# GpSimd instead of VectorE for the subtraction that makes wo_l, in an attention and softplus feed-forward kernel on one Trainium2 core

## The chip, the cores and the metric

The kernel runs on one core of a Trainium2 chip. The metric is the device time of one execution in microseconds (us). An engine is named as in the profile: PE is TensorE's matmul (PEld its weight load), DVE is VectorE, ACT is ScalarE, POOL is GpSimd, SP is SyncE, which only issues DMAs here.

## The reference

Eight batches of eight heads, with 576 rows of 64. A first softmax attention lets 32 packed queries p look at k and v; a second one lets q look at the 32 packed results. The heads are put side by side, which gives x of 4608 rows and 512 columns, and a feed-forward part with softplus follows.

```python
p_packed = sm_attn(p, k, v)
out = sm_attn(q, p_packed, p_packed)
x = attn_out.transpose(0, 2, 1, 3).reshape(B * S, H * D)
h = x @ w_in                                        # 512 x 2048
g = np.maximum(h, 0.0) + np.log1p(np.exp(-np.abs(h)))
return (g @ w_out).astype(np.float32)               # 2048 x 512
```

The weights w_in and w_out are float64; everything else is float32.

## The kernel before

**The work.** For each batch b the attention is computed first. Its last products aT (the weights of the second softmax) are split into a rounded high part at_h (ScalarE, L545) and a low part at_l (VectorE, L546). The feed-forward part runs over 16 slices f of 128 columns of w_in; one (b, f) is called a unit. `make_m` multiplies the packed results into w_in (PE psm, L563) and splits the product into mh (ScalarE, L578) and ml (VectorE, L579); for batch 0 one call serves two units. `gemm1` (PE ph, L600) makes h of the unit in two halves of 288 columns with three products, high by high, high by low and low by high. `softplus` takes |h| (ScalarE L622), exp (L624), ln (L625), adds max(h, 0) (VectorE L627, reading PSUM), lets GpSimd copy the last 64 columns aside (L631) and splits the rest into gh (VectorE L614) and gl (L615). Two units later `gemm2_tile` (L638) adds gh·wo_h, gh·wo_l and gl·wo_h into PSUM. The unit f+1 of gemm1 overwrites the PSUM that L627 of unit f has read, so PE waits for it.

**The conversion.** The float64 weights are turned into float32 bits on the chip, in the generator `convert`, one step for each of 16 slices of w_in (i0 to i15) and 16 of w_out (o0 to o15), in the order i0 i1 o0 o1 i2 i3 o2 o3 and so on. A step has these instructions, all on tiles of 128x512:

- a DMA of the float64 slice into one of four places (L156, on SP's queue)
- ScalarE makes m from the high words (L200) and r from the low words (L204)
- VectorE makes t from m in two instructions (L206: the sign; L211: shift and or)
- GpSimd adds t and r as integers (L219), which rounds; for w_in the sum goes to w_in_sb, for w_out it stays in r
- for w_out only: ScalarE rounds t to wo_h (L238), and the subtraction r - wo_h makes wo_l (L244)

The tiles m, r and t come from rings of one or two buffers, in the first steps also from the softplus tiles. So the r of a later step (L204, on ScalarE) has to wait until the last reader of an earlier r is done: the add for w_in, the subtraction for w_out.

**What sets the order.** PE's order is the program's own. On the other engines a scheduler puts the instructions of the generators in order when the program is built; each engine then runs its queue strictly in that order. The main loop calls `next(conv)` by the numbers CONV_EARLY, CONV_THEN and CONV; attention and softplus of the next unit are called in between, so the conversion's steps stand among theirs on every engine. All conversion is done within the first batch.

Of the kernel before, what the change touches and what calls it, by code (L numbers as in the profile page):

```python
# [26 lines left out]
def pack_attention_then_softplus_ffn(  # L27
# [10 lines left out]
    nc = tc.nc  # L38
# [110 lines left out]
    def load64(srcs, nm, place):  # L149
        if place is None:  # L150
            x = cv.tile([P, CN], I64, tag="x", name=f"x_{nm}", bufs=2)
        else:
            x = rest[:, place:place + 8, :].rearrange("x f j -> x (f j)").bitcast(I64)
        n = P // len(srcs)
        for i, src in enumerate(srcs):
            nc.sync.dma_start(  # L156
                x[i * n:(i + 1) * n].rearrange("x (a n) -> x a n", a=src.shape[1]), src
            )
        return x
# [13 lines left out]
    def convert(order):  # L173

        srcs = {"i": w_in_src, "o": w_out_src}

        places, until = [None, None, LAG, LAG + 8], [len(order), len(order), 6, 16]  # L180
        xs, ts, rs, at = {}, {}, {}, {}

        def prefetch(place):
            n = len(at)
            if n < len(order):
                w, i = order[n]
                at[n] = place
                xs[n] = load64(srcs[w](i), f"{w}{i}", places[place])

        def first(n):  # L190
            x = xs.pop(n)
            lo = x.bitcast(U32).rearrange("x (n two) -> x n two", two=2)[:, :, 0]
            hi = x.bitcast(I32).rearrange("x (n two) -> x n two", two=2)[:, :, 1]
            pool, tm, tr, tt = (work, "gh", "gl", "gh") if spare and n % 2 else (cv, "m", "r", "t")

            m = pool.tile([P, CN], F32, tag=tm, name=f"m_{n}", bufs=LAG + 1 if pool is work else 1)
            nc.scalar.activation(m, hi.bitcast(F32), AF.Copy, scale=2.0**-112)  # L200


            r = pool.tile([P, CN], I32, tag=tr, name=f"r_{n}", bufs=LAG + 1 if pool is work else 2)
            nc.scalar.activation(r, lo, AF.Copy, scale=2.0**-29)  # L204
            t = pool.tile([P, CN], I32, tag=tt, name=f"t_{n}", bufs=LAG + 1 if pool is work else 2)
            nc.vector.tensor_scalar(t, m.bitcast(I32), -0x80000000, None, op0=ALU.bitwise_and)  # L206
            ts[n], rs[n] = (t, m), r

        def second(n):
            t, m = ts[n]  # L210
            nc.vector.scalar_tensor_tensor(  # L211
                t, m.bitcast(I32), 3, t, op0=ALU.logical_shift_left, op1=ALU.bitwise_or
            )
            w, i = order[n]
            dst, a = rs[n], 1
            if w == "i":
                dst, a = w_in_sb.bitcast(I32)[:, :, i * P:(i + 1) * P], DM // P
            v = [y.rearrange("x (a n) -> x a n", a=a) for y in (t, rs[n])]
            nc.gpsimd.tensor_tensor(  # L219
                dst if a > 1 else dst.rearrange("x (a n) -> x a n", a=a), *v, op=ALU.add  # L220
            )

        for n in range(2):
            prefetch(n)
        yield
        for n in range(2, 4):
            prefetch(n)
        yield
        for n in range(len(order) + 1):
            if n < len(order):  # L230
                first(n)
                if n < until[at[n]]:
                    prefetch(at[n])
            yield
            w, i = order[n - 1] if n else ("i", 0)
            t = ts.pop(n - 1)[0].bitcast(F32) if n else None
            if w == "o":
                nc.scalar.copy(wo_h[:, i, :], t)  # L238
            yield
            if n < len(order):  # L240
                second(n)
            yield
            if w == "o":
                nc.vector.tensor_tensor(  # L244
                    wo_l[:, i, :], rs[n - 1].bitcast(F32), wo_h[:, i, :].bitcast(F32),
                    op=ALU.subtract,
                )
                yield
# [452 lines left out]

    pt = load_pack(0, (nc.sync, nc.scalar))
    conv = convert(order)
    for g in range(G):
        load("k", 0, g)
# [112 lines left out]
```

## Time and profile before

| | |
|---|---|
| median of 3 runs | 772.86 us (772.16 to 773.06) |
| the profiled execution's own time | 772.16 us |
| its span, first to last instruction | 770.4 us |
| granted TensorE clock, mean | 0.98 |
| PE busy | 730.1 us, 95% |
| VectorE, ScalarE, GpSimd busy | 530.7, 433.4, 98.7 us |
| the 16 subtractions L244 on VectorE | between 32.9 and 144.1 us from the span's start |

Times in the profile are us from the start of the span, unless marked ns. A row of the timeline is: start, duration, engine, line, operation, output<-input, shapes, and in brackets the engine's idle time before it with what ended it; where a row is followed by x2, the duration is that of both together. A row of the groups is: line, engine, operation, out<-in, shapes, count | busy us, mean ns of one | idle us before, and what ended it. A row of the waits is: who waited <- for whom: us in total, times, the longest. A row of the stretches is: from:to and length, then busy us (and instructions) of PE, PEld, DVE, ACT and POOL, the granted clock, the DMA engines' share, GB/s. A row with min/median/max gives these durations in ns.

### The profile page before, as it was taken

Reading aid. Unit: us, or ns where it says so; the run is one execution under the profiler, and the core shown is the slowest. Engines: PE = TensorE matmul, PEld = TensorE weight load, DVE = VectorE, ACT = ScalarE, POOL = GpSimd, SP = SyncE. Lnnn points to the kernel's source line nnn. Section 1 sums busy time; section 2 is a strip of 40 time slices with the busy share of each in tenths; the row PEclk is TensorE's granted clock in tenths of the full one; section 3 lists DMA queues with packets and bytes.
Section 4 is the critical chain, followed back from the end, with each engine's and each line's share of the span. In section 5 each row is a group of like instructions: output and inputs, shape, how many; then the busy total and the mean of one; then the engine's idle time right before and its main releaser. Section 6 shows DMA issues by size and latency. Waiting matters only on the chain.

```text
span 770.4 us, 14175 instructions
## 1 busy us (share of the span) xinstructions
PE 730.1 (95%) x5360; PEld 579.0 (75%) x5360; DVE 530.7 (69%) x1092; ACT 433.4 (56%) x1057; POOL 98.7 (13%) x166
## 2 busy tenths in 40 slices
PE   6557998999999999999999999999999999999997
PEld 4335776787787877887788877877887877888886
DVE  2696879975787568675877568675877558665554
ACT  5667977665555455565455355565555364555540
POOL 1143444200000000000000000000000000000110
PEclk9957999999999999999999999999999999999999
DMA  9877755534312144033312134033312210010002
GB/s 210 231 192 171 180 149 134 123 73 74 65 31 71 30 64 92 1 94 62 68 26 70 31 63 93 1 86 62 63 32 60 40 31 1 1 55 1 1 1 69
DMA packets 149668, 55.97 MB, mean 73 GB/s; under 512 B 116320, under 2 KB 142944, under 8 KB 149600
## 3 DMA queue, kind: packets, MB, share of 16 engines
q1 hardware_dynamic: 149328, 55.00, 32.1%
q8 instruction: 42, 0.69, 0.4%
q14 instruction: 26, 0.21, 0.1%
q10 hardware_dynamic: 272, 0.07, 0.0%
HBM read 45.61 MB, written 9.44 MB: 71 GB/s over the span
## 4 chain that ended last, share of the span: by engine, by line
PE 83%; DVE 6%; ACT 5%; DMA 4%; issue 1%; POOL 1%; SPq 0%; ACTq 0%; DVEq 0%; POOLq 0%
PE acc L638 41%; PE ph L600 26%; PE acc_m L638 6%; PE psm L563 4%; PE ps L277 3%; DMA rest<-in_moe_w_out 2%; DVE at_l L546 1%; PE ps L320 1%; PE psa L312 1%; DMA x_i<-in_moe_w_in 1%; ACT e L624 1%; DVE e L627 1%; ACT m L200 1%; ACT e L622 1%; DVE t L206 1%
## 5 line engine op out<-in xcount | busy, mean ns | idle before, releaser
L638 PE MATMUL acc<-wo_h,gh 128*128 128x512 f32 x512 | 207.7, 406 | 0.0
L627 DVE SCALAR_TENSOR_TENSOR e<-ph,e 128x288 f32<-128x288 f32 x256 | 114.1, 454 | 133.4 <-ACT e L625 130.7
L622 ACT ACTIVATE e<-ph 128x288 f32<-128x288 f32 x256 | 103.0, 403 | 179.5 <-PE ph L600 155.0
L638 PE MATMUL acc<-wo_l,gh 128*128 128x512 f32 x512 | 201.4, 393 | 0.0
L638 PE MATMUL acc<-wo_h,gl 128*128 128x512 f32 x512 | 201.1, 393 | 0.0
L600 PE MATMUL ph<-at_h,mh 128*128 128x288 f32 x512 | 158.5, 309 | 13.1 <-ACT at_h L545 7.2
L600 PE MATMUL ph<-at_l,mh 128*128 128x288 f32 x512 | 153.4, 300 | 3.7 <-DVE at_l L546 3.7
L600 PE MATMUL ph<-at_h,ml 128*128 128x288 f32 x512 | 152.8, 299 | 0.0
L600 PEld LDWEIGHTS ph<-at_h,mh 128*128 128x128 f32 x512 | 97.7, 191 | 48.0 <-DVE gl L615 15.1
L631 POOL COPY rest<-e 128x64 f32<-128x64 f32 x128 | 53.3, 417 | 575.7 <-DVE e L627 542.9
L638 PEld LDWEIGHTS acc<-wo_h,gh 128*128 128x128 f32 x512 | 96.4, 188 | 26.9 <-issue 12.3
L638 PEld LDWEIGHTS acc<-wo_h,gl 128*128 128x128 f32 x512 | 96.3, 188 | 21.2
L624 ACT ACTIVATE e<-e 128x288 f32<-128x288 f32 (+1 forms) x240 | 109.4, 456 | 3.9
L625 ACT ACTIVATE e<-e 128x288 f32<-128x288 f32 (+1 forms) x240 | 109.3, 456 | 3.0
L638 PEld LDWEIGHTS acc<-wo_l,gh 128*128 128x128 f32 x512 | 96.6, 189 | 13.1
L600 PEld LDWEIGHTS ph<-at_l,mh 128*128 128x128 f32 x512 | 97.9, 191 | 8.4 <-DVE at_l L546 5.3
L600 PEld LDWEIGHTS ph<-at_h,ml 128*128 128x128 f32 x512 | 97.9, 191 | 0.0
L615 DVE TENSOR_TENSOR gl<-e,gh 128x512 fp32r<-128x512 f32 x128 | 87.6, 684 | 6.3
L578 ACT CAST mh<-psm 128x512 fp32r<-128x512 f32 (+1 forms) x72 | 36.3, 540 | 60.8 <-PE psm L563 60.6
L614 DVE CAST gh<-e 128x512 fp32r<-128x512 f32 x128 | 55.5, 434 | 5.9
L579 DVE TENSOR_TENSOR ml<-psm,mh 128x512 fp32r<-128x512 f32 (+1 forms) x72 | 43.0, 624 | 22.0 <-ACT mh L578 21.8
L563 PE MATMUL psm<-w_in_sb,pt 64*32 64x512 f32 (+1 forms) x576 | 40.9, 560 | 8.2 <-ACT T_k L269 4.8
(84 smaller groups left out, 694.8 us busy)
## 6 DMA issues: line engine op xcount, KB each, us to landing
v<-in_v SPq DMA_DIRECT2D x16, 576.0 KB, 5.4
x_i<-in_moe_w_in SPq DMA_DIRECT2D x28, 256.0 KB, 4.5
k<-in_k SPq DMA_DIRECT2D x48, 144.0 KB, 3.3
q<-in_q SPq DMA_DIRECT2D x48, 144.0 KB, 3.4
x_o<-in_moe_w_out SPq DMA_DIRECT2D x11, 512.0 KB, 3.7
out<-o SPq DMA_DIRECT2D x18, 256.0 KB, 2.5
rest<-in_moe_w_out SPq DMA_DIRECT2D x5, 512.0 KB, 6.2
k<-in_k SPq DMA_DIRECT2D x4, 576.0 KB, 6.1
```

Of the source, the lines that this page charges most:

```text
L563: nc.tensor.matmul(ps[hh * J:(hh + 1) * J, :n], res["pt"][g][o:o + D, hh * J:(hh + 1) * J], w_in_sb[o:o + D, hh, c * n:(c + 1) * n], start ...
L578: nc.scalar.copy(mh[:, cols], ps[:, :n])
L579: nc.vector.tensor_tensor(ml[:, cols], ps[:, :n], mh[:, cols].bitcast(F32), op=ALU.subtract)
L600: nc.tensor.matmul(ph[:, :C], x[:, ms], y[:, g, cs], start=(i == 0), stop=(i == 3 * G - 1),)
L614: nc.vector.tensor_copy(hi, x)
L615: nc.vector.tensor_tensor(lo, x, hi.bitcast(F32), op=ALU.subtract)
L622: nc.scalar.activation(es[c], hv[c], AF.Abs)
L624: nc.scalar.activation(x, x, AF.Exp, scale=-1.0)
L625: nc.scalar.activation(x, x, AF.Ln, bias=1.0)
L627: nc.vector.scalar_tensor_tensor(es[c], hv[c], 0.0, es[c], op0=ALU.max, op1=ALU.add)
L631: nc.gpsimd.tensor_copy(rest[:, rest_at(b, f), r:r + REST], e[:, NT * P:])
L638: nc.tensor.matmul(acc, x[:, cs], y[:, f, :], start=(first and i == 0), stop=(last and i == 2),)
```

## The change

The subtraction r - wo_h is issued on GpSimd instead of VectorE. Operands and result are the same.

```diff
             if w == "o":
-                nc.vector.tensor_tensor(
+                nc.gpsimd.tensor_tensor(
                     wo_l[:, i, :], rs[n - 1].bitcast(F32), wo_h[:, i, :].bitcast(F32),
                     op=ALU.subtract,
                 )
```

The scheduler sets the order anew. PE's queue has the same order as before, the others don't. In the rows below, - is before and + is the changed program; a number behind a name tells buffers apart. First VectorE, at the end of the first attention: a, z and aT are the second softmax's, at_l_522 the low part that the first gemm1 needs; t_286 belongs to i3, t_334 to o2, t_363 to o3, r_216 to o1.

```order
 L378 STREAM_TRANSPOSE aT_1_493<-a_0_1_470 128x576
-L244 TENSOR_TENSOR wo_l<-r_216,wo_h 128x512
-L206 TENSOR_SCALAR t_286<-m_282 128x512
-L546 TENSOR_TENSOR at_l_522<-aT_1_493,at_h_521 128x576
 L211 SCALAR_TENSOR_TENSOR t_286<-m_282,t_286 128x512
 L206 TENSOR_SCALAR t_334<-m_330 128x512
 L206 TENSOR_SCALAR t_363<-m_359 128x512
+L546 TENSOR_TENSOR at_l_522<-aT_1_493,at_h_521 128x576
 L211 SCALAR_TENSOR_TENSOR t_334<-m_330,t_334 128x512
 L211 SCALAR_TENSOR_TENSOR t_363<-m_359,t_363 128x512
-L244 TENSOR_TENSOR wo_l<-r_332,wo_h 128x512
```

The second at_l moved behind L211 of i3 and both L206 of o2 and o3. GpSimd at the same place, with r_189 of o0, t_244 of i2 and r_332, r_361 of o2 and o3:

```order
 L219 TENSOR_TENSOR r_216<-t_218,r_216 128x512
+L244 TENSOR_TENSOR wo_l<-r_189,wo_h 128x512
+L244 TENSOR_TENSOR wo_l<-r_216,wo_h 128x512
 L219 TENSOR_TENSOR w_in_sb<-t_244,r_242 128x4x128
 L219 TENSOR_TENSOR w_in_sb<-t_286,r_284 128x4x128
 L219 TENSOR_TENSOR r_332<-t_334,r_332 128x512
 L219 TENSOR_TENSOR r_361<-t_363,r_361 128x512
+L244 TENSOR_TENSOR wo_l<-r_332,wo_h 128x512
+L244 TENSOR_TENSOR wo_l<-r_361,wo_h 128x512
```

The subtractions come in pairs behind a pair of adds. ScalarE a little later, where softplus of unit 0 (e_0_541) runs; r_559 and m_557 belong to i5, r_581 and m_579 to o4, T_k to the next batch's attention:

```order
+L622 ACTIVATE e_0_541<-ph_0_1_534 128x288
+L204 ACTIVATE r_559<-x_i_288 128x512
+L624 ACTIVATE e_0_541<-e_0_541 128x576
+L200 ACTIVATE m_557<-x_i_288 128x512
 L625 ACTIVATE e_0_541<-e_0_541 128x576
+L204 ACTIVATE r_581<-rest 128x512
+L200 ACTIVATE m_579<-rest 128x512
 L269 COPY T_k_0_0_555<-psT_k_0_0_551 128x288
-L200 ACTIVATE m_557<-x_i_288 128x512
-L204 ACTIVATE r_559<-x_i_288 128x512
 L269 COPY T_k_0_1_577<-psT_k_0_1_573 128x288
```

The r of i5 moved ahead of softplus 0's exp, and m of o4 ahead of both copies T_k. Last, VectorE around softplus of unit 11 (e_11_1490), in the changed program alone, where a, z and aT are of the next batch's second softmax and t_1446 is of i14:

```order
L374 TENSOR_TENSOR a_1_0_1369<-a_1_0_1369,z_1_0_1506 128x576
L206 TENSOR_SCALAR t_1446<-m_1442 128x512
L378 STREAM_TRANSPOSE aT_0_1511<-a_1_0_1369 128x576
L211 SCALAR_TENSOR_TENSOR t_1446<-m_1442,t_1446 128x512
L627 SCALAR_TENSOR_TENSOR e_11_1490<-ph_11_0_1476,e_11_1490 128x288
```

and before:

```order
L206 TENSOR_SCALAR t_1446<-m_1442 128x512
L372 TENSOR_SCALAR z_1_0_1506<-z_1_0_1506 128x18
L211 SCALAR_TENSOR_TENSOR t_1446<-m_1442,t_1446 128x512
L373 RECIPROCAL z_1_0_1506<-z_1_0_1506 128x18
L244 TENSOR_TENSOR wo_l<-r_1386,wo_h 128x512
L627 SCALAR_TENSOR_TENSOR e_11_1490<-ph_11_0_1476,e_11_1490 128x288
```

L374 and L378, which stood behind L627 of unit 11, now stand ahead of it.

## The prediction

> **What bounds the kernel now.** The page gives the span and the busy times, the stretches say where TensorE isn't full, and the waits of TensorE say for what.
>
> ```profile
> span 770.4 us, 14175 instructions
> PE 730.1 (95%) x5360; PEld 579.0 (75%) x5360; DVE 530.7 (69%) x1092; ACT 433.4 (56%) x1057; POOL 98.7 (13%) x166
> ```
>
> ```profile
> 20.00:60.00 40.00, 21.57 (x180) 15.45 (x180) 30.16 (x55) 26.02 (x53) 13.66 (x11) 0.70 0.84 211
> 60.00:150.00 90.00, 82.61 (x653) 61.61 (x654) 77.47 (x159) 71.33 (x150) 36.40 (x35) 0.96 0.62 153
> 150.00:770.00 620.00, 613.89 (x4411) 493.87 (x4409) 417.58 (x864) 325.06 (x831) 45.62 (x113) 1.00 0.23 48
> ```
>
> From 150 us TensorE is busy 613.89 of 620 us; nothing of the edit is left there. The 16 edited instructions lie in 33 to 144 us. In 20 to 150 us TensorE is idle 18.43 + 7.39 = 25.8 us: only by these idle times, and by the granted clock (0.70 in the first stretch), can the edit move the end. VectorE is the busiest feeder (77.47 of 90 us), GpSimd has room on the average (36.40 of 90). TensorE's waits in 30 to 70 us, then in 70 to 150 us:
>
> ```profile
> PE ph L600 <- ACT at_h L545: 7.2, 2, 6.7
> PE psm L563 <- ACT T_k L269: 4.8, 2, 2.8
> PE ph L600 <- DVE e L627: 2.8, 1, 2.8
> PE ph L600 <- DVE at_l L546: 2.5, 2, 2.2
> ...
> PE ph L600 <- DVE e L627: 3.1, 4, 1.8
> PE psm L563 <- POOL w_in_sb L219: 1.7, 1, 1.7
> ```
>
> So the waits end on the softmax's last products (at_h, at_l), on ScalarE's copies and on softplus (e), all of which stand in queues that the conversion shares.
>
> **The change, part by part.** *What is removed and added.* The groups in 30 to 150 us:
>
> ```profile
> L244 DVE TENSOR_TENSOR wo_l<-r,wo_h 128x512 fp32r<-128x512 f32 x16 | 14.3, 899 | 1.9 <-POOL r L219 1.7
> ...
> L206 DVE TENSOR_SCALAR t<-m 128x512 int32<-128x512 int32 x29 | 16.6, 576 | 6.7 <-ACT m L200 6.6
> ```
>
> VectorE is rid of 16 x 899 ns = 14.3 us and of 1.9 us of waits. GpSimd gets 16 subtractions of 128x512. No fp32 subtraction of that size runs there now; the nearest row is its own add in front of it:
>
> ```profile
> L219 POOL TENSOR_TENSOR r<-t,r x15: 1266/1296/1657, 31.5 to 142.5; 128x512 int32<-128x512 int32 x15
> ```
>
> I take 1.3 us, since operands, size and place are the same. Bounds: 0.63 us, VectorE's fastest subtraction (627 ns), below; two adds, 2.6 us, above. At 1.3 us GpSimd goes to 36.4 + 14 x 1.3 = 55 of 90 us. That would be hidden, if the two engines didn't hinder each other. They do:
>
> ```profile
> 31.50 1.66 POOL L219 TENSOR_TENSOR r<-t,r 128x512 int32<-128x512 int32 x1 [1.84 <-ACT T_q L269]
> 39.82 1.65 POOL L219 TENSOR_TENSOR w_in_sb<-t,r 128x512 int32<-128x512 int32 x1 [6.67 <-DVE t L211]
> 45.09 1.33 POOL L219 TENSOR_TENSOR w_in_sb<-t,r 128x512 int32<-128x512 int32 x1 [3.62 <-DVE t L211]
> 47.45 2.81 POOL L219 TENSOR_TENSOR r<-t,r 128x512 int32<-128x512 int32 x2 [1.03 <-DVE t L211]
> ```
>
> ```profile
> 35.36 0.74 DVE L363 TENSOR_TENSOR a<-a,m 128x576 f32<-128x576 f32 x1
> ...
> 39.59 0.75 DVE L374 TENSOR_TENSOR a<-a,z 128x576 f32<-128x576 f32 x1
> 40.26 1.82 DVE L546 TENSOR_TENSOR at_l<-aT,at_h 128x576 fp32r<-128x576 f32 x1
> ...
> 42.00 0.76 DVE L378 STREAM_TRANSPOSE aT<-a 128x576 f32<-128x576 f32 x1
> 42.70 0.64 DVE L244 TENSOR_TENSOR wo_l<-r,wo_h 128x512 fp32r<-128x512 f32 x1
> 43.27 0.41 DVE L206 TENSOR_SCALAR t<-m 128x512 int32<-128x512 int32 x1
> 43.60 0.74 DVE L546 TENSOR_TENSOR at_l<-aT,at_h 128x576 fp32r<-128x576 f32 x1
> 44.27 0.68 DVE L211 SCALAR_TENSOR_TENSOR t<-m,t 128x512 int32<-128x512 int32 x1
> 44.87 1.83 DVE L206 TENSOR_SCALAR t<-m 128x512 int32<-128x512 int32 x2
> 46.62 1.28 DVE L211 SCALAR_TENSOR_TENSOR t<-m,t 128x512 int32<-128x512 int32 x2
> 49.07 1.74 DVE L244 TENSOR_TENSOR wo_l<-r,wo_h 128x512 fp32r<-128x512 f32 x1 [1.17 <-POOL r L219]
> ```
>
> The add of 39.82 ran until 41.47; at_l, which takes 0.74 us elsewhere, began at 40.26 and ended at 42.08, 0.6 us behind the add. Likewise the second L206 of 44.87 ends at 46.70, after the add of 45.09 to 46.42, and L244 of 49.07 at 50.81, after 50.26. So a VectorE instruction on SBUF alone that meets a GpSimd add waits until it ends, and GpSimd waits the other way (the 1.65). Ahead of softplus and of copies from PSUM this doesn't show. The Trainium skill's page "SBUF — State Buffer", section "Who interferes with whom", says the same: the shared port pair goes whole to whichever began first, if VectorE has two SBUF inputs or its two-port mode. By that rule the removed 14.3 us aren't won; what stretched L244 now stretches its neighbours.
>
> *Early stage, by the changed order.* (1) The two first subtractions run on GpSimd behind the add of 31.50, which ends at 33.16, at about 33.4 to 36.0; VectorE's L363 of 35.36 meets the second: +0.6 us on the chain to aT. (2) L211 of i3, formerly behind the second at_l, now stands before it, and with it both L206 of o2 and o3. It releases GpSimd's add, the second L206 waits that add out (the pattern of 44.87, 1.83 us for two), and at_l behind it too. From aT to at_l's start were 0.57 + 0.34 = 0.9 us; now 0.6 + 0.34 + 1.2 + 0.35 = 2.5. So TensorE's ph starts its second half 0.6 + 1.6 = 2.2 us later. (3) ScalarE's r of i5 takes the buffer that the subtraction of o2 frees, and now stands ahead of the exp of softplus 0:
>
> ```profile
> 47.17 0.68 ACT L624 ACTIVATE e<-e 128x576 f32<-128x576 f32 x1
> ...
> 53.09 0.38 ACT L269 COPY T_k<-psT_k 128x288 f32<-128x288 f32 x1
> ```
>
> at_l ends at 46.5, L211 of o2 at 47.1, two adds on GpSimd end at about 50.1, the subtraction of o2 at 51.7, so r ends at 52.3 and the exp that began at 47.17 begins then. Behind it stand m, Ln, r and m (0.6 us each, two waiting for VectorE and GpSimd in turn), and the second T_k, which ended at 53.47, ends near 56.9: TensorE, which waits for it (the 4.8 us above), starts unit 1 3.4 us late. What speaks for the change is in (3) as well: L206 no longer stands behind the wo_l of 49.07, which cost 1.17 + 1.74 us; I have counted it, its place is empty in the new queue. (4) Before softplus 1 ScalarE's m of o5 is out of the way and VectorE's L211 too: -0.8, so 2.6. (5) For softplus 3, m and r of i7 go ahead of both L622 and r of o7 behind Ln; these rows held e:
>
> ```profile
> 72.40 0.67 ACT L204 ACTIVATE r<-rest 128x512 int32<-128x512 uint32 x1
> ...
> 75.25 0.67 ACT L204 ACTIVATE r<-x_o 128x512 int32<-128x512 uint32 x1
> 75.80 0.68 ACT L625 ACTIVATE e<-e 128x576 f32<-128x576 f32 x1
> ```
>
> Two of them, some 1.1 us less, out of a TensorE wait of 1.8 us (the longest of the four above). Left: 2.6 - 1.1 = **+1.5 us**; +0.3 if at_l isn't held, +3.5 if each meeting costs a full add more.
>
> *Middle, 78 to 120 us.* Softplus sits close to ScalarE's queue, and there little is reordered; one TensorE wait of the four on e, 0.4 us, I let go: **-0.4**.
>
> *Late stage.*
>
> ```profile
> 124.01 0.69 DVE L211 SCALAR_TENSOR_TENSOR t<-m,t 128x512 int32<-128x512 int32 x1
> ...
> 127.29 0.63 DVE L244 TENSOR_TENSOR wo_l<-r,wo_h 128x512 fp32r<-128x512 f32 x1
> 127.83 0.81 DVE L627 SCALAR_TENSOR_TENSOR e<-ph,e 128x288 f32<-128x288 f32 x2
> 128.56 1.10 DVE L374 TENSOR_TENSOR a<-a,z 128x576 f32<-128x576 f32 x1
> ```
>
> Now L374 and L378 stand ahead of L627 of softplus 11, and four GpSimd instructions (two adds, two subtractions) fall where VectorE needs its own: L615, L374 and L206 wait about 1.2, 0.9 and 1.1 us. L374 and L378 are 1.4 us more, wo_l 0.6 less; some 1.1 us of the waits fall in idle time: L627 2.9 us later, and TensorE with it. In return the 1.7 us wait on w_in_sb goes, since m of i15 is ahead of softplus 12: +1.2. Softplus 13 may lose more (0 to 2 us: L366, L211 and L255 are now ahead of it). I take **+1.2**.
>
> *Sum:* 1.5 - 0.4 + 1.2 = +2.3 us on the profiled execution, whose own time is 772.16 us (span 770.4 and 1.8 around it): 774.5. The median of the runs shown, 772.86, is 0.7 above it, so **775.2 us**.
>
> **Rivals.** *A: VectorE's relief wins (faster).* For it: 14.3 us off the busiest feeder, no more waiting of VectorE for GpSimd's add (1.17 us at 49.07), and the i15 wait. Against it: the three stretched rows above. It decides if the second L206 of (2) gets in before the add, or doesn't wait for it; then at_l is at most 0.4 us late, T_k gains the 2 us that L206 stood behind L244, less that, and the late wait of 1.7 goes: 772.9 + 0.4 - 2.0 - 1.7 = **769.6 us**. The Trainium skill's "GPSIMD Engine Reference", section 4.1, speaks against A: it sends two-input elementwise work to VectorE, GpSimd being about half as fast; 1296 against 688 ns agree.
> *B: the stages cancel.* Half of (2) and (3) is taken up by waits there already (7.2 and 4.8 us above), and the late stage returns it: **772.9 us**.
> *C: GpSimd becomes the bound.* If the subtraction takes 2.6 us, GpSimd needs 36.4 + 14 x 2.6 = 73 of 90 us, and its r buffers hold up ScalarE in every pair: three subtractions stand in the early chain, 3 x 1.3 = 3.9 us more: **779.1 us**.
> *D: the clock is released earlier.*
>
> ```profile
> 64.00:66.00 2.00, 2.00 (x14) 1.25 (x16) 0.62 (x2) 1.16 (x3) 0.00 (x0) 0.50 0.43 154
> 66.00:68.00 2.00, 2.00 (x22) 1.14 (x22) 1.07 (x3) 1.32 (x3) 0.24 (x1) 0.86 0.00 0
> ```
>
> The granted clock (the column behind GpSimd's) stood at 0.50 up to 66 us, and TensorE was busy all of 64 to 66. 2 us of work at 0.50 are 1 us at full clock, so a release two such stretches earlier would win 2 us, one later lose them: 775.2 - 2 = **773.2 us**, the other side being inside the range. The Trainium skill's "TensorE: Matmul & The Clock Gate" (What's actually happening) has it released after a busy window of about 3.4 us whose phase is free; one run here can't show the phase.
>
> **How the numbers follow.** A measurement tells about 0.2%, 1.5 us, from no change. My forecast has 0.45, C 0.12, A 0.22, B 0.15, D 0.06 (same). Faster by over 0.2% is A: 0.22. Same is B and D and a little of the forecast's lower end: 0.22. Slower: 0.56. The likeliest case alone runs from 773.3 (early +0.3) to 778.5 (early +3.5, late +3.2 with softplus 13). The range, 770.5 to 779.2 us, takes in B, D and C's time and leaves out half of A and what is beyond C.
>
> **What would show it.** Right: the subtraction at 1.3 us on GpSimd; the second at_l 2 us later than 43.60; the exp of softplus 0 at 51 to 53 us instead of 47.17; VectorE's L206 and L374 with maxima over 1.5 us in more places; the TensorE wait on w_in_sb gone and the one on e before unit 12 longer. Wrong: at_l before 44.5 us and T_k before 52 us (A); a subtraction above 2 us (C); TensorE idle in 20 to 150 us not above 25.8 us would refute the whole sum.

## The result and the profile after

The changed kernel takes 780.59 us (median of 6 runs, 778.26 to 781.56) beside 772.33 us for the kernel before on the same chip (6 runs): ratio 1.0108, 95% interval 1.0093 to 1.0122, so slower by 1.1% or 8.3 us. The prediction said 775.2 us, 770.5 to 779.2: the sign was right, the size under a third of what came, and the time lies 1.4 us above the range. The profiled execution took 779.66 us, 7.5 us more than the 772.16 us of before, and the two spans differ by the same 7.5 us.

The page:

```profile
span 777.9 us, 14196 instructions
PE 730.3 (94%) x5360; PEld 580.3 (75%) x5360; DVE 533.5 (69%) x1076; ACT 433.8 (56%) x1057; POOL 119.3 (15%) x182
```

VectorE lost 16 instructions and is busy 2.8 us longer, not 14.3 us shorter. The three stretches:

```profile
20.00:60.00 40.00, 19.21 (x169) 14.45 (x170) 29.60 (x50) 24.50 (x49) 19.25 (x15) 0.59 0.84 210
60.00:150.00 90.00, 78.64 (x620) 59.69 (x619) 76.35 (x140) 68.82 (x146) 51.52 (x47) 0.95 0.59 144
150.00:770.00 620.00, 617.84 (x4444) 496.36 (x4443) 420.58 (x869) 329.50 (x839) 46.08 (x114) 1.00 0.23 49
```

TensorE is idle 20.79 + 11.36 = 32.2 us in 20 to 150 us, against 25.8 before. The granted clock in 60 to 150 us is 0.95 where it was 0.96, though TensorE left the first half clock at 61.56 us instead of 66.58: two new stretches at half clock, of 3.4 us each, came behind it (64.98 to 68.38 and 126.42 to 129.82). TensorE's waits in 30 to 70 us:

```profile
PE ph L600 <- ACT at_h L545: 8.0, 2, 7.5
PE psm L563 <- ACT T_k L269: 6.8, 1, 6.8
PE ph L600 <- DVE at_l L546: 3.9, 2, 2.2
```

and in 70 to 150 us:

```profile
PE ph L600 <- DVE e L627: 5.5, 3, 2.7
PE psm L563 <- DVE pt L342: 1.3, 1, 1.3
```

The wait on w_in_sb (1.7 us) is gone, as predicted; the waits on softplus (e) grew from 3.1 to 5.5 us, and that on pt (the packed results, which VectorE's L342 copies out of PSUM for psm) from 0.4 to 1.3. Where VectorE's relief went is in the groups of 30 to 150 us, after and then before:

```profile
L211 DVE SCALAR_TENSOR_TENSOR t<-m,t 128x512 int32<-128x512 int32 x29 | 23.7, 820 | 0.3
L244 POOL TENSOR_TENSOR wo_l<-r,wo_h 128x512 fp32r<-128x512 f32 x16 | 22.7, 1425 | 1.9 <-ACT wo_h L238 0.9 <-DVE gh L614 0.4
L206 DVE TENSOR_SCALAR t<-m 128x512 int32<-128x512 int32 x29 | 20.4, 706 | 7.2 <-ACT m L200 6.0 <-POOL w_in_sb L219 0.9
L615 DVE TENSOR_TENSOR gl<-e,gh 128x512 fp32r<-128x512 f32 x14 | 12.7, 909 | 0.1
```

```profile
L211 DVE SCALAR_TENSOR_TENSOR t<-m,t 128x512 int32<-128x512 int32 x29 | 19.7, 681 | 0.3
L615 DVE TENSOR_TENSOR gl<-e,gh 128x512 fp32r<-128x512 f32 x15 | 10.1, 675 | 0.0
```

The same work in three groups takes 4.0 (L211), 3.8 (L206, 576 to 706 ns) and 14 x 0.234 = 3.3 us (L615) longer: 11.1 of the 14.3 us came back as longer VectorE instructions. Before, L211 never took over 0.70 us; now the longest takes 1.79. That it is GpSimd's subtraction that lengthens L211 is seen in two experiments below, f2 and f4: with the new order but no subtraction on GpSimd, L211 takes 0.68 us in the mean, as before.

**Where the 7.5 us arose.** A unit starts with its first product ph (TensorE's rows of L600). Time between two such starts in us; the other columns belong to experiments below:

| unit to unit | before | after | f1 GpSimd, old order | f2 VectorE, new order | f4 none, new order | h7 mixed order |
|---|---|---|---|---|---|---|
| 0 to 4 | 37.71 | 38.56 | 37.27 | 38.47 | 36.50 | 35.59 |
| 4 to 10 | 38.26 | 38.38 | 39.86 | 38.87 | 37.72 | 38.78 |
| 10 to 11 | 7.14 | 8.26 | 7.16 | 9.21 | 8.03 | 7.15 |
| 11 to 12 | 5.90 | 8.78 | 5.80 | 7.82 | 7.58 | 5.90 |
| 12 to 13 | 8.01 | 6.30 | 8.77 | 6.29 | 6.30 | 7.47 |
| 13 to 14 | 4.81 | 7.29 | 5.87 | 7.39 | 6.18 | 4.85 |
| 14 to 16 | 10.91 | 10.77 | 11.61 | 12.33 | 10.78 | 10.91 |

Unit 0 starts 1.2 us later (40.53 instead of 39.32), units 0 to 10 take 1.0 us more, **units 10 to 16 take 41.4 instead of 36.8 us, 4.6 more**, and the rest of the span 0.7. How far one trace can be trusted is told by c1, c2 and c3 below, which up to unit 12 are the kernel before, in the same order: their unit 0 starts at 38.03 to 39.62 us, units 0 to 4 take 36.39 to 37.72 us, 4 to 10 38.30 to 39.50, 10 to 12 13.04 to 13.32 (13.04 before). So up to unit 10 a difference of 1 us between two traces says little; from 10 to 12 it counts. These are TensorE's rows there, each with the idle time ahead of it; before first:

```profile
121.86 0.64 PE L563 MATMUL psm<-w_in_sb,pt 64*32 64x256 f32 x8 [0.40 <-DVE pt L342]
128.33 0.40 PE L600 MATMUL ph<-at_h,mh 128*128 128x288 f32 x1 [0.69 <-DVE e L627]
135.75 0.67 PE L563 MATMUL psm<-w_in_sb,pt 64*32 64x256 f32 x16 [1.65 <-POOL w_in_sb L219]
141.15 0.40 PE L600 MATMUL ph<-at_h,mh 128*128 128x288 f32 x1 [0.21 <-DVE e L627]
```

```profile
125.17 0.64 PE L563 MATMUL psm<-w_in_sb,pt 64*32 64x256 f32 x8 [1.27 <-DVE pt L342]
134.51 0.40 PE L600 MATMUL ph<-at_h,mh 128*128 128x288 f32 x1 [2.06 <-DVE e L627]
148.10 0.40 PE L600 MATMUL ph<-at_h,mh 128*128 128x288 f32 x1 [2.66 <-DVE e L627]
```

And this is VectorE's and GpSimd's timeline ahead of 134.51 and 148.10 in the changed kernel:

```profile
123.03 1.26 POOL L219 TENSOR_TENSOR r<-t,r 128x512 int32<-128x512 int32 x1 [1.93 <-DVE t L211]
...
129.21 1.29 POOL L219 TENSOR_TENSOR r<-t,r 128x512 int32<-128x512 int32 x1 [2.95 <-DVE t L211]
130.57 1.30 POOL L244 TENSOR_TENSOR wo_l<-r,wo_h 128x512 fp32r<-128x512 f32 x1
...
143.36 1.77 POOL L244 TENSOR_TENSOR wo_l<-r,wo_h 128x512 fp32r<-128x512 f32 x1 [0.34 <-ACT wo_h L238]
```

```profile
123.60 1.31 DVE L363 TENSOR_TENSOR a<-a,m 128x576 f32<-128x576 f32 x1
124.84 0.28 DVE L342 COPY pt<-psx 128x128 f32<-128x128 f32 x1
...
129.33 1.21 DVE L372 TENSOR_SCALAR z<-z 128x18 f32<-128x18 f32 x1
...
130.87 1.62 DVE L374 TENSOR_TENSOR a<-a,z 128x576 f32<-128x576 f32 x1
132.41 0.41 DVE L206 TENSOR_SCALAR t<-m 128x512 int32<-128x512 int32 x1
132.75 0.77 DVE L378 STREAM_TRANSPOSE aT<-a 128x576 f32<-128x576 f32 x1
133.44 0.64 DVE L211 SCALAR_TENSOR_TENSOR t<-m,t 128x512 int32<-128x512 int32 x1
134.01 0.80 DVE L627 SCALAR_TENSOR_TENSOR e<-ph,e 128x288 f32<-128x288 f32 x2
...
143.90 1.79 DVE L211 SCALAR_TENSOR_TENSOR t<-m,t 128x512 int32<-128x512 int32 x1
145.61 0.74 DVE L579 TENSOR_TENSOR ml<-psm,mh 128x256 fp32r<-128x256 f32 x2
146.28 0.73 DVE L371 TENSOR_REDUCE z<-a 128x18 f32<-128x576 f32 x1
146.94 0.76 DVE L255 STREAM_TRANSPOSE k<-k 128x576 f32<-128x576 f32 x1
147.63 0.78 DVE L627 SCALAR_TENSOR_TENSOR e<-ph,e 128x288 f32<-128x288 f32 x2
```

VectorE has no gap from 129.33 to 134.8 and from 142.8 to 148.4. Its queue is the path here: what stands ahead of L627, and how long GpSimd holds it, goes to TensorE. L363 ends at 124.9, behind the add of 123.03 to 124.29, and pt behind it; L372, which works on 128x18 elements, waits the add of 129.21 out; L374 the subtraction of 130.57 to 131.87; L211 of 143.90 the subtraction of 143.36 to 145.13. The first two are held by adds that GpSimd made before as well: in f2 and f4, where it makes no subtraction, L363 takes 1.34 and 1.32 us and L372 1.20 us in both. So these two holds come with the new order, those of L374 and L211 with the moved subtraction.

Ahead of 148.10 ScalarE's queue is close behind. Its Ln of softplus 13 (L625) stands behind wo_h, which waits for the held L211, and ends at 146.92; VectorE's queue then costs the last 0.7 us up to L627:

```profile
145.72 0.62 ACT L238 CAST wo_h<-t 128x512 fp32r<-128x512 f32 x1 [0.60 <-DVE t L211]
146.25 0.68 ACT L625 ACTIVATE e<-e 128x576 f32<-128x576 f32 x1
```

### The profile page after: what moved, and what is told of

The parts are those of the page before. It is cut to its first block, busy times and chain, and to the rows that moved or that the text cites. A ratio compares the mean times of both kernels' runs of the same rounds, so it can differ in the third digit from the quotient of the medians.

```text
span 777.9 us, 14196 instructions
## 1 busy us (share of the span) xinstructions
PE 730.3 (94%) x5360; PEld 580.3 (75%) x5360; DVE 533.5 (69%) x1076; ACT 433.8 (56%) x1057; POOL 119.3 (15%) x182
## 4 chain that ended last, share of the span: by engine, by line
PE 77%; DVE 3%; ACT 2%; issue 0%; POOL 0%; DVEq 0%; ACTq 0%
PE acc L638 40%; PE ph L600 24%; PE acc_m L638 6%; PE psm L563 4%; PE ps L277 2%; PE ps L320 1%; PE psa L312 1%; DVE at_l L546 1%; ACT e L624 1%; ACT e L622 0%; DVE e L627 0%; ACT at_h L545 0%; DVE t L211 0%; ACT e L625 0%; DVE q L255 0%
## 5 line engine op out<-in xcount | busy, mean ns | idle before, releaser
L627 DVE SCALAR_TENSOR_TENSOR e<-ph,e 128x288 f32<-128x288 f32 x256 | 114.0, 454 | 137.3 <-ACT e L625 135.8
L622 ACT ACTIVATE e<-ph 128x288 f32<-128x288 f32 x256 | 102.8, 403 | 182.4 <-PE ph L600 155.8
L600 PE MATMUL ph<-at_h,mh 128*128 128x288 f32 x512 | 158.4, 309 | 15.9 <-ACT at_h L545 8.0
L600 PE MATMUL ph<-at_l,mh 128*128 128x288 f32 x512 | 153.7, 300 | 5.1 <-DVE at_l L546 5.1
L600 PE MATMUL ph<-at_h,ml 128*128 128x288 f32 x512 | 153.1, 299 | 0.0
L600 PEld LDWEIGHTS ph<-at_h,mh 128*128 128x128 f32 x512 | 97.9, 191 | 50.2 <-DVE gl L615 14.2
L625 ACT ACTIVATE e<-e 128x288 f32<-128x288 f32 (+1 forms) x240 | 109.3, 455 | 2.9
L600 PEld LDWEIGHTS ph<-at_l,mh 128*128 128x128 f32 x512 | 98.1, 192 | 9.9 <-DVE at_l L546 6.7
L600 PEld LDWEIGHTS ph<-at_h,ml 128*128 128x128 f32 x512 | 98.2, 192 | 0.0
L615 DVE TENSOR_TENSOR gl<-e,gh 128x512 fp32r<-128x512 f32 x128 | 90.8, 710 | 6.8 <-DVE gh L614 0.5
L614 DVE CAST gh<-e 128x512 fp32r<-128x512 f32 x128 | 56.6, 442 | 6.2
```

What stands on the lines that cost most here:

```text
L600: nc.tensor.matmul(ph[:, :C], x[:, ms], y[:, g, cs], start=(i == 0), stop=(i == 3 * G - 1),)
L614: nc.vector.tensor_copy(hi, x)
L615: nc.vector.tensor_tensor(lo, x, hi.bitcast(F32), op=ALU.subtract)
L622: nc.scalar.activation(es[c], hv[c], AF.Abs)
L625: nc.scalar.activation(x, x, AF.Ln, bias=1.0)
L627: nc.vector.scalar_tensor_tensor(es[c], hv[c], 0.0, es[c], op0=ALU.max, op1=ALU.add)
```

## The experiments

The theories. H (hold): GpSimd's second instruction on SBUF holds VectorE's. O (order): the new order of VectorE's and ScalarE's queues costs, not GpSimd. K (clock): waits bring TensorE's half clock back. Differences below are the ratio's, on 772 us.

### By part and by stage

**e1, e2.** Only some of the subtractions move.

```diff
-                nc.vector.tensor_tensor(
+                (nc.gpsimd if i >= 10 else nc.vector).tensor_tensor(
```

> Only the subtractions of o10 to o15 are GpSimd's, those of o0 to o9 stay on VectorE. Theory H (hold): GpSimd's second instruction on SBUF holds VectorE's instructions that stand ahead of softplus 11 and 13; the changed kernel lost 4.8 us between the first product psm of units 10/11 (108.83 us before, 110.95 us after) and that of batch 1 (145.69 and 152.62), so this kernel comes out near 772.3 + 4.8 = 777 us, with no loss before 108 us. Theory K (clock): 1.5 to 2 us of that is the half clock of 126 to 130 us, which may not come again when TensorE arrives earlier: 775 us. Theory E (early): the cost is made early and only carried on: at most 773 us.

Measured: 1.0092 (1.0077 to 1.0108), +7.1 us. The second has the condition turned round, so that o0 to o9 are GpSimd's:

> Only the subtractions of o0 to o9 are GpSimd's, those of o10 to o15 stay on VectorE. Theory H: the early part is what the milestones of the changed kernel show until 117 us, +2.2 us, so 774.5 us; this is also the first term of the prediction (+1.5 to +1.1). Theory E: nearly all of the loss, 779 us or more. If the sum of this kernel's and the late kernel's differences isn't near 8 us, the stages act on each other.

Measured: 1.0089 (1.0073 to 1.0105), +6.9 us. Both miss, and their sum, 14.0 us, isn't 8.3. The second kernel starts unit 10 only 1.7 us later than before, as H said, and then loses 6.3 us between units 10 and 16, where VectorE makes the subtractions again. (Its trace is of the slowest execution, 780.79 us beside a median of 777.86, with a stretch of 6.8 us at half clock from 145.54 on.) What the two have in common is the late order: both depart from VectorE's order of before around softplus 10 to 13 (places 164 to 211 of its queue in the one, 172 to 211 in the other). Stage by stage can't be told apart with the scheduler in between.

**e3.** Neither engine makes the subtraction.

```diff
-                nc.vector.tensor_tensor(
-                    wo_l[:, i, :], rs[n - 1].bitcast(F32), wo_h[:, i, :].bitcast(F32),
-                    op=ALU.subtract,
-                )
+                pass
...
-        for i, (x, y) in enumerate(((gh, wo_h), (gh, wo_l), (gl, wo_h))):
+        for i, (x, y) in enumerate(((gh, wo_h), (gh, wo_h), (gl, wo_h))):
```

> The subtraction is left out on both engines and the product with wo_l takes wo_h again, so TensorE has the same work and the output lacks the low part. VectorE has the same relief as in the changed kernel, and the scheduler may put other work in its places, but GpSimd has no second instruction. Theory H: without GpSimd's instruction the relief can be seen: 769 to 771.5 us, faster than before. Theory O (order): the loss comes from the new order of VectorE's and ScalarE's queues that the missing subtractions bring: 775 us or more here too.

Measured: 0.9999 (0.9989 to 1.0009), no difference. That isn't O's; 771.49 us stands just inside H's numbers, but isn't faster than before, as H said. Unit 10 starts 3.2 us earlier than before, and units 10 to 16 take 2.6 us more.

**e4.** Both engines make it.

```diff
-                nc.vector.tensor_tensor(
-                    wo_l[:, i, :], rs[n - 1].bitcast(F32), wo_h[:, i, :].bitcast(F32),
-                    op=ALU.subtract,
-                )
+                for eng, j in ((nc.vector, i), (nc.gpsimd, i + 2 if i < 14 else i)):
+                    eng.tensor_tensor(
+                        wo_l[:, j, :], rs[n - 1].bitcast(F32), wo_h[:, i, :].bitcast(F32), op=ALU.subtract
+                    )
```

> VectorE keeps its subtraction, and GpSimd makes the same difference a second time, into the place of a wo_l that is written for good two steps later. So GpSimd's load and its hold on the r buffers are those of the changed kernel, without VectorE's relief. Theory H: at least as slow as the changed kernel, 780 to 786 us. Theory O: the order stays near that of before, 772 to 775 us.

Measured: 1.0163 (1.0149 to 1.0176), +12.6 us, inside H's range. GpSimd's part is dear by itself; but here too the scheduler made another order.

### Order and engine apart

The order was then pinned: after the program is made, each instruction of a list is tied behind the one ahead of it on its engine. The lists are VectorE's and ScalarE's rows of before ("old") or of the changed kernel ("new"), over the stretch in which the two differ.

```diff
             pack_attention_then_softplus_ffn(tc, *args)
+            pin(nc, tc)
...
+def pin(nc, tc):
+    made = {i.name: i for i in nc.cur_bb.bb.instructions}
+    how = mybir.DependencyInfo(mybir.DependencyClass.NoSync, mybir.DependencyReason.DATA)
+    for row in ROWS:
+        for x, y in zip(row, row[1:]):
+            tc.add_manual_dep(made[f"I-{y}"], f"I-{x}", how, reason="row")
```

f1 is the changed kernel with the old rows:

> The subtraction is GpSimd's, but VectorE's and ScalarE's queues are pinned to the order of before, with the subtractions taken out of VectorE's; the order of all other instructions is then that of before on every engine. Theory H (hold): GpSimd's second instruction by itself holds VectorE and the r buffers; 776 to 781 us. Theory O (order): only the new order costs, so this kernel has the relief alone: 769 to 773 us.

f2 is the kernel before with the new rows:

> The subtraction stays on VectorE, but VectorE's and ScalarE's queues are pinned to the order of the changed kernel (12 of VectorE's places near the end of the conversion and some DMA issues differ). Theory O: the new order costs what the changed kernel lost: 778 to 782 us. Theory H: the order alone costs little, 772 to 776 us.

f3 is e3 with the old rows:

> The subtraction is left out on both engines (the product with wo_l takes wo_h, so the output lacks the low part), and all queues have the order of before. Both theories: the relief of 14.3 us of VectorE's time alone: 768 to 771.5 us. If it is 771.7 or more, VectorE's time for the subtraction lies in idle time, and the relief on which rival A rests is worth nothing.

f4 is e3 with the new rows:

> The subtraction is left out on both engines (the product with wo_l takes wo_h), and all queues have the order of the changed kernel, so that against the changed kernel only GpSimd's 16 subtractions are missing. Theory H: without them the loss is gone, 769 to 773 us. Theory O: the loss stays, 776 us or more.

Measured, as difference to before with its interval:

| subtraction by | old order | new order |
|---|---|---|
| nobody | f3: -2.5 us (0.9954 to 0.9979) | f4: -0.2 us (0.9984 to 1.001) |
| VectorE | 0 (the kernel before) | f2: +9.0 us (1.0104 to 1.0131) |
| GpSimd | f1: +3.9 us (1.0039 to 1.0064) | +8.3 us (the changed kernel) |

f1 comes out at 775.23 us, just under H's range and above O's; f2 is O's, f3 both's, f4 H's. Neither theory alone stands. With the old order the move costs 3.9 us; the new order costs 9.0 us with no move at all. And they don't add up: with the new order it makes no measurable difference which engine subtracts (+9.0, +8.3), but if nobody does, the loss is gone (-0.2). Read along the rows, the new order costs 2.3 us where nobody subtracts, 9.0 us where VectorE does and 4.4 us where GpSimd does. (f2 isn't quite the new order, since 12 of VectorE's places differ; and its trace has a stretch at half clock behind softplus 13, 146.64 to 150.06, which the changed kernel's doesn't: units 14 to 16 take 12.33 us instead of 10.77.) In the new order VectorE's queue is the path around softplus 11 and 13; there a subtraction of its own (0.68 us) and a hold by GpSimd's (0.9 to 1.1 us) cost alike. f2 has two subtractions in the 4 us ahead of softplus 13's L627, where the changed kernel has the one hold; VectorE's rows:

```profile
142.85 0.68 DVE L244 TENSOR_TENSOR wo_l<-r,wo_h 128x512 fp32r<-128x512 f32 x1
...
144.78 0.68 DVE L244 TENSOR_TENSOR wo_l<-r,wo_h 128x512 fp32r<-128x512 f32 x1
...
146.07 0.78 DVE L627 SCALAR_TENSOR_TENSOR e<-ph,e 128x288 f32<-128x288 f32 x2
```

f3 shows that VectorE's relief is real, 2.5 us; f1 that GpSimd's part takes 6.4 us (2.5 + 3.9) in its place. A hold in the middle of f1, on GpSimd, VectorE and ScalarE:

```profile
76.58 1.48 POOL L244 TENSOR_TENSOR wo_l<-r,wo_h 128x512 fp32r<-128x512 f32 x1
76.82 1.79 DVE L211 SCALAR_TENSOR_TENSOR t<-m,t 128x512 int32<-128x512 int32 x1
78.64 0.62 ACT L238 CAST wo_h<-t 128x512 fp32r<-128x512 f32 x1 [1.51 <-DVE t L211]
```

L211 waits the subtraction out, ScalarE's wo_h stands behind L211, and the second L622 of softplus 4 (79.16) behind wo_h. Units 4 to 10 take 1.6 us more than before; TensorE has two waits there that before doesn't have, 0.86 us for T_k (ended at 80.62) and 0.84 us for ml (100.08).

### The places

h1, h5 and h6 are the changed kernel with the old rows only in part: from softplus 9 on, around softplus 10 and 11, from softplus 12 on (the lists of f1 over VectorE's places 149 to 213, 149 to 177 and 178 to 213, and ScalarE's 163 to 215, 163 to 189 and 190 to 215; elsewhere the new rows). On VectorE around softplus 11, which h1 and h5 change:

```diff
-    L372 z, L373 z, L374 a, L206 t, L378 aT, L211 t, L627 e of softplus 11, L614 gh
+    L206 t, L372 z, L211 t, L373 z, L627 e of softplus 11, L374 a, L614 gh, L378 aT
```

> GpSimd makes the subtraction; queues as in the changed kernel until softplus 9, from there on VectorE's and ScalarE's are pinned to the order of before. Theory P (places): what the changed kernel loses late, 41.4 us from unit 10 to unit 16 instead of 36.8, is half the order; with the order of before and GpSimd's subtraction these units took 39.2 us, so 2.2 us come back: 778.4 us. Theory I (idle carried in): the late loss comes from arriving later, and stays: 780 us or more.

Measured: 1.0048 (1.0035 to 1.0061), +3.7 us, so 4.6 us come back, twice what P said. It is as good as f1: all of the new order's loss is late, and its early part costs nothing in the end.

> The changed kernel with the order of before only around softplus 10 and 11 (178 - 149 = 29 places of VectorE, 27 of ScalarE), so that L374 and L378 stand behind L627 of softplus 11 again. Theory P: unit 11 to 12 takes 5.8 to 6.5 us instead of 8.8, and with it goes the half clock that came at 126 us; the wait for w_in_sb before unit 13 gives 0 to 1 us back: 777.5 to 778.5 us. Theory I: no change, 780 us or more.

Measured: 1.0058 (1.0041 to 1.0076), +4.5 us, 3.8 us back; 777.09 us, a little under P. Unit 11 to 12 takes 5.80 us instead of 8.78, and no half clock comes at 126 us. But the wait on softplus 13 stays (2.86 us, ended at 143.90), and here the clock falls behind it (144.14 to 147.56): units 13 to 16 take 20.0 us instead of 18.1. In this trace units 10 to 16 are thus only 1.1 us shorter than in the changed kernel's.

> The changed kernel with the order of before only from softplus 12 on. Theory P: unit 13 to 14 takes 5 to 5.9 us instead of 7.3, but m and r of i15 are behind softplus 12 again, which brings back 1 to 1.7 us of waiting for w_in_sb before unit 13: 779.5 to 781 us. If it is below 778.5, softplus 13 was the dearer place of the two.

Measured: 1.0088 (1.0074 to 1.0103), +6.8 us: 779.46 us, as P said, though its interval touches that of the changed kernel. Unit 13 to 14 falls from 7.29 to 4.47 us, unit 12 to 13 rises from 6.30 to 9.51. The late wait for w_in_sb comes back with the old order there. By the medians softplus 11 was the dear place.

h7 puts the better pieces together, with VectorE's subtraction: old rows early and late, new rows from softplus 2 to 9, and i15 early. Around the last, on VectorE:

```diff
 L615 gl of softplus 11
+L206 t of i15
+L211 t of i15
 L255 k, twice
 L627 e of softplus 12
-L206 t of i15
 L627 e of softplus 12
-L211 t of i15
```

> Candidate for a better kernel: the subtraction stays on VectorE, early and late queues are those of before; between softplus 2 and softplus 9 the order is that of the changed kernel, which took 44.3 us from unit 3 to unit 10 instead of 45.3, and m, r and t of i15 stand ahead of softplus 12, so that the wait for w_in_sb of 1.65 us before unit 13 goes. Theory P: 769 to 770.5 us. If the order only shifts waits: 771.5 us or more.

Measured: 0.998 (0.9969 to 0.9991), 1.5 us faster than before (770.62 us, 12 runs), just above P's range: a version that beats both, by a little. In the trace the gain is between units 0 and 4 (2.1 us) and at unit 13 (0.5 us), and units 4 to 10 take 0.5 us more. Of the 2.1 us some 1.3 can be that one execution: c2 and c3 below, in the order of before, take 1.0 and 1.3 us less than the trace of before there.

### The clock

In f1 TensorE waited 2.35 us for w_in_sb ahead of unit 13 (1.65 before), and its clock fell to half behind that. Its row, with the idle time ahead of it:

```profile
136.55 0.73 PE L563 MATMUL psm<-w_in_sb,pt 64*32 64x256 f32 x16 [2.35 <-POOL w_in_sb L219]
```

The stretch behind it, where before has 1.00 in the column of the clock:

```profile
138.00:140.00 2.00, 2.00 (x10) 2.00 (x9) 1.97 (x4) 0.84 (x2) 1.92 (x2) 0.50 0.01 1
```

To lengthen that one wait, and nothing else if the scheduler leaves the order as it is, GpSimd's add of i15 is made again in part, in the kernel before: a quarter (c2), half (c3, 2 in place of 1), all (c1, 4).

```diff
-            nc.gpsimd.tensor_tensor(
-                dst if a > 1 else dst.rearrange("x (a n) -> x a n", a=a), *v, op=ALU.add
-            )
+            d = dst if a > 1 else dst.rearrange("x (a n) -> x a n", a=a)
+            for s in [slice(None)] + [slice(0, 1)] * ((w, i) == ("i", 15)):
+                nc.gpsimd.tensor_tensor(d[:, s], *(y[:, s] for y in v), op=ALU.add)
```

> The kernel before with one quarter of GpSimd's add of i15 made a second time, so that TensorE's wait for w_in_sb before unit 13 grows from 1.65 to about 2.0 us; nothing else moves. Theory K (a wait of over some 2.2 us drops the clock): no half clock, +0.4 us: 772.3 us. Theory N (the clock has nothing to do with it): the same +0.4 us.

> As the quarter, with half of the add of i15 made again: the wait grows to about 2.35 us. Theory K: a half clock of some 3.4 us behind it, +0.7 us for the wait and +1.1 to +1.7 us for the clock: 773.6 to 774.2 us. Theory N: +0.7 us, 772.6 us.

> As the quarter, with the whole add of i15 made again: the wait grows to about 2.95 us. Theory K: +1.3 us for the wait and +1.1 to +1.7 us for a half clock of 3.4 us: 774.3 to 774.9 us. Theory N: +1.3 us, 773.2 us.

| | wait before unit 13 | units 13 to 14 | ratio | difference |
|---|---|---|---|---|
| before | 1.65 us | 4.81 us | 1 | 0 |
| c2 | 2.25 us | 5.93 us | 1.0017 (1.0003 to 1.0031) | +1.3 us |
| c3 | 2.53 us | 5.73 us | 1.0017 (1.0005 to 1.003) | +1.3 us |
| c1 | 3.07 us | 7.32 us | 1.0038 (1.0026 to 1.005) | +2.9 us |

All three traces show a half clock of 3.4 us behind the wait, where before has none; c2's too, which K had not expected at 2.0 us (it became 2.25). In c2 and c3, whose queues have the order of before, units 13 to 14 take 1.1 and 0.9 us longer: about 1 us for the half clock. c1 is no clean case. There the scheduler changed the order too: m, r and L366 stand between softplus 13's exp (141.56) and its Ln (143.84) on ScalarE, which before follow each other directly, and c1's 7.32 us hold a further wait of 1.29 us on that softplus. So c1's 2.9 us, which lie in K's range (2.4 to 3.0) and not at N's 1.3, can't be put down to the clock alone. c2's 1.3 us are more than either had expected, c3's lie between K and N, and their intervals, about 1 us to each side, take in both. That the clock falls behind such a wait is shown by the traces; what it costs in the time isn't shown to better than a microsecond. Last, h8 is h7 with GpSimd's subtraction (`nc.gpsimd` in place of `nc.vector`, old and new rows mixed as there), where the add of i15 comes early:

> GpSimd's subtraction with the mixed order that was 1.5 to 1.8 us better than before with VectorE's; there the add of i15 comes early and the wait before unit 13 is gone. Theory K: with that wait goes the half clock behind it, and GpSimd's hold costs only the 1.2 us of unit 4 and small change: 771.5 to 772.5 us. If the hold costs 3.5 us again, 774 us, it isn't tied to that wait.

Measured: 1.0001 (0.9987 to 1.0016), 771.64 us: as K said. Its trace shows no half clock behind 70 us (1.00 in the column behind GpSimd's):

```profile
70.00:150.00 80.00, 74.92 (x604) 56.26 (x597) 73.21 (x135) 66.03 (x138) 47.50 (x42) 1.00 0.66 158
```

Against h7 GpSimd's subtraction costs 1.6 us here, against 3.9 us in the old order. Of the missing 2.3 us, 0.7 are the longer wait for i15 in f1 and about 1 the half clock behind it, which h8 doesn't have; the rest is not assigned, and each of the two costs has an interval of 1 us or more to each side.

## Why the prediction was right in sign and wrong in size

- **The subtraction's price** (1.3 us, from the add ahead of it): right. It takes 1.27 to 1.77 us, in the middle 1.35; rival C (2.6 us) is out.
- **The hold**: right, and the reason why VectorE's 14.3 us weren't won (11.1 us came back in three groups; f3 has the relief at 2.5 us, f1 the hold at 6.4).
- **The early stage, +1.5 us**: most of its steps came, its sum nearly (2.1 us), and that in part by luck. These are ScalarE's rows:

```profile
51.97 0.67 ACT L204 ACTIVATE r<-x_i 128x512 int32<-128x512 uint32 x1 [1.75 <-POOL wo_l L244]
52.54 0.67 ACT L624 ACTIVATE e<-e 128x576 f32<-128x576 f32 x1
...
56.53 0.68 ACT L269 COPY T_k<-psT_k 128x288 f32<-128x288 f32 x2
```

  The r of i5 waits for the subtraction, the exp begins at 52.54 (52.3 predicted), the second T_k ends at 57.2 (56.9). And VectorE's:

```profile
44.48 1.82 DVE L206 TENSOR_SCALAR t<-m 128x512 int32<-128x512 int32 x2
46.22 0.74 DVE L546 TENSOR_TENSOR at_l<-aT,at_h 128x576 fp32r<-128x576 f32 x1
```

  The second at_l comes 2.6 us later than 43.60 behind the two L206 (2 predicted). Step 1 named the wrong instruction (L372 was held, not L363), and step 4 was too kind: unit 2 starts 4.0 us late, not 2.6. Step 5 came: TensorE's wait on softplus 3 falls from 1.82 to 0.73 us. A further 0.9 us came back between units 2 and 3 (7.66 us instead of 8.52), where TensorE's clock rose earlier. No term stood for that, and it is luck: in c1, c2 and c3 these units take 9.02, 7.74 and 7.56 us. Up to unit 4 the sum is 2.1 us, 0.4 of which the run had before the change could act.
- **The middle, -0.4 us**: nothing came of it; units 4 to 10 take 0.1 us more.
- **The late stage, +1.2 us: here it failed; measured +4.6.** One part came as said: the wait on w_in_sb is gone (units 12 to 13: -1.7). L627 of softplus 11 is "2.9 us later" in its amount (units 11 to 12: +2.9), but by other instructions than those named, so that the match is partly luck: L615 and L206 weren't held (0.67 and 0.41 us); L614 was (1.50 us instead of 0.41), L372 and L374, together some 3.0 us beside the 3.2 counted. The failing step is "Softplus 13 may lose more (0 to 2 us ...). I take +1.2", that is, softplus 13 at zero: it lost 2.5 us (units 13 to 14). And one place was not looked at: units 10 to 11 take 1.1 us more, 0.6 of it L363 held by an add ahead of pt. 1.17 + 2.48 + 1.12 - 0.14 (units 14 to 16) = 4.63. L366, L211 and L255 had been seen ahead of softplus 13; what was missing is that VectorE has no gap there, so that they have no idle time to fall into, and that the subtraction holds L211 for 1.1 us, which delays ScalarE's Ln as well.
- **The clock** was taken as an early release only (rival D). A wait of the late stage can also bring the half clock back. In the changed kernel it came in 126.4 to 129.8 us, and lies beside the path: VectorE has no gap from 121.20 us up to softplus 11's L627 at 134.01, and ScalarE's Ln for it had ended at 131.82, so slower products held nothing up there. Where it did cost time is in traces of other kernels (f1, c2, c3, f2, h5).
- **The range**: the bounds of the likeliest case, 773.3 and 778.5, are added to the profiled 772.16, the forecast to the median 772.86; by the same median they are 774.0 and 779.2. The measured time lies outside either way.
- **Rivals**: A's relief is real, but worth 2.5 us and overtaken by the hold; B's cancelling did not happen: nothing came back late. The 8.3 us of the median can be split into 3.9 us for the move in the old order (f1) and 4.4 us for the late part of the new order (h1 gives 4.6 back); since the two don't add up for every engine, this is one way to split them.

## What to carry to other kernels

An instruction moved off a busy engine to one whose instructions hold up those of the first, as GpSimd's hold VectorE's here, comes back as stretched neighbours: count what the neighbours lose before what the engine wins. When a scheduler sits between the code and the queues, the new order can cost as much as the move: pin the old order and test the two apart, and put a stretch without gaps on the feeding engine at full price, each instruction and each hold. Stage-by-stage variants don't isolate a stage if the order elsewhere moves with them, and a single trace doesn't settle a microsecond in a stage that runs at a changing clock.

## What the hardware showed that was not expected

The granted clock changed only at instants on a raster: from 35 us on, wherever the traces of this case let them be read, those of one trace lie whole multiples of 3.41 us apart. In the changed kernel, one-us stretches in which it changes:

```profile
61.00:62.00 1.00, 0.85 (x6) 0.64 (x4) 1.00 (x1) 0.00 (x0) 0.69 (x1) 0.72 1.12 221
68.00:69.00 1.00, 1.00 (x7) 0.86 (x5) 0.00 (x0) 0.32 (x1) 0.00 (x0) 0.81 0.00 0
126.00:127.00 1.00, 1.00 (x7) 1.00 (x7) 1.00 (x3) 1.00 (x3) 0.26 (x1) 0.71 0.00 0
129.00:130.00 1.00, 1.00 (x6) 0.70 (x5) 1.00 (x3) 1.00 (x2) 0.79 (x1) 0.59 1.03 280
```

A mean of 0.72 between 0.50 and 1 means that 0.44 us were at full clock; so the clock rose at 61.56 and 68.38, fell at 126.42 and rose at 129.82. The distances are 6.82, 58.04 and 3.40 us: 2, 17 and 1 times 3.41. So a wait costs whole stretches of 3.4 us at half clock or nothing, by how it lies to the raster. The wait of 2.66 us that ended at 148.10 lies across such an instant (126.42 + 6 x 3.41 = 146.9) and dropped nothing; those of 2.25 to 3.07 us in c2, c3 and c1 did. On the same softplus 13, f2 and h5 waited 2.76 and 2.86 us between two instants of their rasters, and the clock fell at the next one (146.64 and 144.14). The same wait may thus cost more in one execution than in another; repeated traces of one kernel, which would show it, weren't taken. How much of a window has to be idle isn't settled: ahead of the fall at 126.42 TensorE waited 0.76 and 1.27 us, with products psm between them. The Trainium skill's "TensorE: Matmul & The Clock Gate" (What's actually happening) has such a free-running window of about 3.4 us, and the trace agrees; it has the clock fall after an idle window of that length, and here 2.25 us of waiting were enough.

Small instructions pay the hold in full: L372 on 128x18 elements took 1.21 us behind an add in the changed kernel, and 0.15 at 148.34.
